# Reordering the launch and the stretch between attention and MLP, and loading wq and wk in joined rows

## The chip, the cores and the metric

The kernel runs on one core of a Trainium2 chip. The core has a matrix engine, TensorE (PE, with its weight loads shown apart as PEld), three engines for elementwise work, VectorE (DVE), ScalarE (ACT) and GpSimd (POOL), and SyncE (SP), which here only issues transfers between the device memory and the core's memory. The metric is the device time of one execution in microseconds (us), the median over several runs.

## The reference

Two equal layers, each a linear attention block and a GELU MLP, both on a layer-normalized input and with a residual. S = 2048 tokens, D = 448, 16 heads of 28, F = 1792.

```python
_layernorm = (x - mean) / sqrt(var + 1e-5)
phi = lambda t: where(t > 0, t + 1, exp(t)) + 1e-6

def A(x, wqkv, wo):                       # q, k, v = heads of x @ wqkv
    pq, pk = phi(q), phi(k)
    kv  = einsum("bhsd,bhse->bhde", pk, v)
    z   = einsum("bhsd->bhd", pk)
    num = einsum("bhqd,bhde->bhqe", pq, kv)
    den = einsum("bhqd,bhd->bhq", pq, z)[..., None] + 1e-6
    return (num / den) @ wo               # heads joined again

def B(x, w1, b1, w2, b2):
    return gelu(x @ w1 + b1) @ w2 + b2    # tanh form

for layer in range(2):                    # the same weights in both
    x = x + A(layernorm(x), wqkv, wo)
    x = x + B(layernorm(x), w1, b1, w2, b2)
```

## The kernel before

**Tiles.** The 2048 tokens are 16 tiles of 128 rows (index t), in 4 blocks of 4 tiles. The 448 columns are taken in 4 chunks of 128, the last of which covers the remaining 64 rows of a weight. To keep precision, every operand of a large product is split into a "hi" part, rounded to the matmul type fp32r by a copy on ACT, and a "lo" part, the rest, by a subtraction on DVE or POOL; a product is hi·hi, hi·lo and lo·hi. In chunk 3 the 64 rows are stored twice, so that one piece holds hi in the upper half and lo in the lower. Products with wq or wk take 11 matmuls per tile: three for each of chunks 0 to 2 and two for chunk 3 (`proj`, L280).

**Order.** The schedule is written out by hand: each engine takes its instructions in the order in which the program issues them, and waits where an operand or a buffer is not ready. So the order of calls in the program is, engine by engine, the order of the work. All loads and stores are issued on SP's queue, in program order too.

**PSUM.** Of its eight banks, tag "m" has two (products with wk, `psk`; later transposes), tag "h" two (the transposes `tp` of normalized tiles in phase 1, the products with wq, `psq`; later the MLP's first product), and tag "acc" four.

**Launch (L84 to L143, L846 to L866).** SP loads x0, then the four chunks of wk, x1, the four chunks of wq and x2; x3 and x4 follow at the start of phase 1. A chunk is one transfer of 128 rows of 448 words (`load_kq`), the last chunk two of 64 rows. x0 is normalized (`stage_a`: statistics on DVE and the power on POOL; `stage_n`: the norm on DVE and on ACT a copy of the last 64 columns, `tail`), transposed on PE (`stage_b`, L236) and split (`stage_x`: XH on ACT L241, XL on DVE L242). Among this the list at L846 puts the splits of wk (`split_hi` L122, `split_lo` L129 and L132) and of wq. PE runs a few products of ones ahead of it all (`warm_up`).

**Phase 1.** A loop over the 16 tiles issues for each the tokens of `STEP` (`STEP_0` for the first tile of a layer):

| token | work |
|---|---|
| K | product with wk of tile t |
| T, X | transpose and split of tile t+1 |
| a, n | statistics and norm of later tiles |
| kp, kh, kl | phi of k, and its hi and lo part |
| s | hi and lo part of the normalized tile, `xnh` and `xnl` |
| G | 11 matmuls that add x^T·phi(k) of tile t-1 to the four "acc" banks |
| Q | product with wq of tile t |
| qp | phi of q (`eq`, L293 to L299) and its store |
| w | the last chunk of wq's split |
| bg | loads and splits of the MLP's weights |
| tu, tv, sp, ld | turning, spreading and loading of later tiles |

Six of the 16 products with wq are left over for the stretch after phase 1.

**Between attention and MLP.** The string `ORDER` (L467) lists that work, with the same few letters for each layer: m and ms make the matrix from x^T·phi(k) and the weights, qz, qs, tq and qq scale, transpose and split the phi(q) of block 0 (tiles j = 0 to 3), `o` multiplies them (L671 to L673), `la` adds the residual and takes statistics (L691), `lb` normalizes (L199, `xm`) and copies the last columns on ACT (L698), T transposes (L236) and x splits. Between these stand the left-over products Q and their phi Qp (`fill_qphi`: three activations on ACT, among them `ep` at L445, an addition on POOL at L447, and a store), with which PE is kept at work. `pre` issues the loads of phi(q) of block 1 and, in layer 0, of two pieces of the MLP's weights.

**MLP.** For each block, 14 slices of F: `mlp1` (L736 to L740), GELU, split, `mlp2` (L754 to L756), and beside it, on the other engines, the attention output of the next block. In the last block of layer 0 the weights wk and wq are loaded again, in two halves each (`stage_square`), and split whole (`split_kq`, L134) for layer 1.

Of the kernel before, what the change touches and what calls it, by code (L numbers as in the profile page):

```python
# [9 lines left out]
F32 = mybir.dt.float32  # L10
# [12 lines left out]
def linear_attn_mlp_kernel(  # L23
# [12 lines left out]
    pe, act, dve, pool, sp = nc.tensor, nc.scalar, nc.vector, nc.gpsimd, nc.sync  # L36
    x0 = x_in[0]
# [24 lines left out]
    def bank(tag, bufs, name):  # L62
        return psum.tile([128, 512], F32, name=name, tag=tag, bufs=bufs)
# [24 lines left out]
    def stage_piece(src, c, eng, s):  # L88

        if c < 3:  # L90
            eng.dma_start(s, src[c * 128:(c + 1) * 128, :])
        else:
            eng.dma_start(s[0:64], src[TL:D, :])
            eng.dma_start(s[64:128], src[TL:D, :])
        return s

    def load_kq(name, col):
        src = wqkv[:, col:col + D]
        st = [work.tile([128, 1024], F32, name="stg", tag="S", bufs=5) for h in range(2)]
        return [stage_piece(src, c, sp, st[c // 2][:, c % 2 * 512:c % 2 * 512 + D]) for c in range(4)]  # L100

    def stage_square(src):

# [16 lines left out]
    def split_hi(name, c, st):  # L120
        hi = piece(name, c if c < 3 else 6)
        act.copy(hi, st[c])  # L122
        wkq[name, c] = (hi, piece(name, 3 + c)) if c < 3 else hi

    def split_lo(name, c, st, eng):

        if c < 3:
            hi, lo = wkq[name, c]
            eng.tensor_tensor(lo, st[c], f(hi), op=OP.subtract)  # L129
        else:  # L130
            lo = wkq[name, 3][64:128]
            eng.tensor_tensor(lo, st[c][64:128], f(lo), op=OP.subtract)  # L132
# [3 lines left out]
            split_hi(name, c, st)  # L136
            split_lo(name, c, st, pool if c in ((1, 2) if name == "k" else (0, 2)) else dve)

    st_k = load_kq("k", D)
    load_x(0, 1)  # L140
    st_q = load_kq("q", 0)
    load_x(0, 2)


# [4 lines left out]
    def warm_up(n):  # L149
        for i in range(n):  # L150
            pe.matmul(warm[:, :128], ones, ones, start=True, stop=True)
# [125 lines left out]
        dve.tensor_sub(lo.rearrange("p (c i n) -> p c i n", c=4, n=32), x, f(h))  # L277


    def proj(name, key, j):  # L280
        ps = bank("m" if name == "k" else "h", 2, "ps" + name)
        o = ps[:, :D]
        b = blocks[key]
        for c in range(3):
            hi, lo = wkq[name, c]
            pe.matmul(o, b.still(b.hi, j, c), hi, start=(c == 0), stop=False)  # L286
            pe.matmul(o, b.still(b.hi, j, c), lo, start=False, stop=False)  # L287
            pe.matmul(o, b.still(b.lo, j, c), hi, start=False, stop=False)  # L288
        pe.matmul(o, b.still(b.hi, j, 3), wkq[name, 3], start=False, stop=False)
        pe.matmul(o, b.still(b.lo, j, 3), wkq[name, 3], start=False, stop=True)  # L290
        return o

    def phi(o, name, into=None):  # L293
# [62 lines left out]
    def stage_a(l, t):  # L356
        sts[l, t] = ln_stats(xt.pop((l, t)))
# [25 lines left out]
    def stage_x(l, t):  # L383
        key = ("a", l, t // 4)
        if t < TURNED[l]:
            split_x(key, t % 4)
        else:
            split_t(key, t % 4, *block(key).pieces(t % 4))
# [9 lines left out]

    ko = {}

    def stage_k(l, t):
        ko[l, t] = proj("k", ("a", l, t // 4), t % 4)

    def stage_kphi(l, t):
        o = ko.pop((l, t))
# [44 lines left out]
    def stage_g(l, t, acc):  # L450
# [16 lines left out]

    ORDER = (
# [4 lines left out]
    )  # L473
    DEFER = NT - ORDER.split().count("Q")

    STEP = "qp K T X s a kp n kh tu kl tv G bg Q ld sp"
    STEP_0 = "K T X w a kp kh n kl s Q bg ld sp", "K T X s kp kh kl a n tu Q ld sp"
    NORM = (
        ((2,), (3, 4), (5, 6), (7,), (8,), (9,), (10,), (11,), (12, 13), (14,), (15,)),
        ((5,), (6,), (7,), (8,), (9,), (10,), (11,), (12, 13), (14,), (15,)),  # L480
# [11 lines left out]
    def phase1(l, tr):  # L492
        za = consts.tile([128, D], F32, name="za", tag="za")
        acc = [bank("acc", 4, f"G{c}")[:, :D] for c in range(4)]
        for t in range(NT):
            norm = NORM[l][t] if t < len(NORM[l]) else ()
            if t == 0:
                load_to(l, NORM[l][1][-1])
            for tok in (STEP if t else STEP_0[l]).split():
                if tok == "sp":  # L500
                    for u in norm:
                        if u % 2:
                            stage_sp(l, u)
                elif tok == "ld" and t + 2 < len(NORM[l]):
                    load_to(l, NORM[l][t + 2][-1])
                elif tok == "a":
                    for u in norm:
                        stage_a(l, u)
                elif tok == "n":
                    for u in norm:  # L510
                        stage_n(l, u)
                elif tok == "tu":
                    for u in norm[:1]:
                        stage_t(l, u)
                elif tok == "tv":
                    for u in norm[1:]:
                        stage_t(l, u)
                elif tok == "w":
                    split_hi("q", 3, st_q)
                    split_lo("q", 3, st_q, dve)  # L520
                elif tok == "T" and t + 1 < NT:
                    stage_b(l, t + 1)
                elif tok == "X" and t + 1 < NT and (l == 0 or t + 1 >= 4):
                    stage_x(l, t + 1)
                elif tok == "K":
                    stage_k(l, t)
                elif tok == "qp":
                    stage_qphi()
                elif tok == "kp":
                    stage_kphi(l, t)  # L530
                elif tok == "kh":
                    stage_kh(l, t)
                elif tok == "kl":
                    stage_kl(l, t, za)
                elif tok == "s":
                    stage_s(l, t)
                elif tok == "G" and t >= 1:
                    stage_g(l, t - 1, acc)
                elif tok == "bg" and l == 0:
                    background(BG[t])  # L540
                elif tok == "Q" and t < DEFER:
                    stage_q(l, t)
            if l == 0 and t == 4:
                sp.dma_start(b1s, b1.rearrange("(c p) -> p c", p=128))
                sp.dma_start(b2b, b2[None, :].to_broadcast([128, D]))
            if t == 11:
                tr.wv = stage_square(wqkv[:, 2 * D:])
            if t == 13:
                trans_load(l, tr)
        return za, acc  # L550
# [300 lines left out]
    split_lo("k", 1, st_k, pool)  # L851
    stage_b(0, 0)
    warm_up(2)
    stage_x(0, 0)
    split_hi("k", 2, st_k)
    split_lo("k", 2, st_k, dve)
    split_hi("k", 3, st_k)
    split_lo("k", 3, st_k, pool)
    stage_a(0, 1)
    split_hi("q", 0, st_q)  # L860
    split_hi("q", 1, st_q)
    stage_n(0, 1)
    split_lo("q", 0, st_q, dve)
    split_lo("q", 1, st_q, dve)
    split_hi("q", 2, st_q)
    split_lo("q", 2, st_q, pool)  # L866

    for l in range(LAYERS):
        tr = SimpleNamespace(mp={})
# [90 lines left out]
```

## Time and profile before

| | |
|---|---|
| median of 3 runs | 883.67 us (883.59 to 883.87) |
| the profiled execution's own time | 883.35 us |
| its span in the profile | 881.6 us |
| granted TensorE clock, mean | 0.999 |
| PE, PEld | 873.2 us (99%), 773.7 us (88%) |
| DVE, ACT, POOL | 483.8 us (55%), 345.3 us (39%), 219.0 us (25%) |
| moved by DMA | 93.71 MB, 106 GB/s in the mean |

The span runs from the first to the last recorded instruction; the execution's time has a little around it. A share is busy time over the span, as a mean over all stages. In the quoted rows of the timeline stand the start in us, the mean duration of one, the engine, the line of the kernel, the operation, out<-in by the program's names, the shapes and a count; in brackets how long the engine stood idle before it and what it had waited for. In rows of the windows stand the window, its length, and for PE, PEld, DVE, ACT and POOL the busy us with the number of instructions, then the granted clock, the busy share of the DMA engines, which counts transfers in flight on each, and GB/s. Rows that begin with a transfer's direction come from the list of DMA issues: count, size of each, and the median us from issue to landing.

### The profile page before, as it was taken

The page shows a single profiled execution, that of the slowest core. Times are in us where ns is not written, and L with a number is a line of the kernel's source. Part 1 is how long each engine was busy: PE and PEld are TensorE (multiplying, and loading weights), DVE is VectorE, ACT ScalarE, POOL GpSimd, SP SyncE. Part 2 cuts the span into 40 slices and gives each one's busy share as a digit, 9 for nine tenths or more (in the row PEclk, how much of TensorE's full clock was granted, in tenths as well). Part 3 has the DMA queues.
Part 4 walks back from the last instruction along what each step waited for, and adds up shares of the span by engine and source line. Part 5 has one row for each costly group of instructions (what it writes and reads, how often), then busy time and mean ns, then how long its engine had stood idle before and what let it go on. Part 6 is the DMA issues. An engine that isn't in the chain of part 4 may idle for free.

```text
span 881.6 us, 11685 instructions
## 1 busy us (share of the span) xinstructions
PE 873.2 (99%) x4190; PEld 773.7 (88%) x4190; DVE 483.8 (55%) x946; ACT 345.3 (39%) x607; POOL 219.0 (25%) x251
## 2 busy tenths in 40 slices
PE   8999999999999999999999999999999999999998
PEld 7999988888888888888899999788888888888887
DVE  6778585658455543226477866755574473432112
ACT  5677645323223322333355664442232233223221
POOL 4366632335012102011222333220220140140000
PEclk9999999999999999999999999999999999999999
DMA  5477733624313402051145543143332323111001
GB/s 177 131 214 233 201 94 119 194 80 140 132 59 104 155 0 96 1 178 48 48 144 188 158 138 95 63 150 102 100 117 90 110 76 132 48 49 42 1 1 42
DMA packets 62762, 93.71 MB, mean 106 GB/s; under 512 B 8816, under 2 KB 57968, under 8 KB 62704
## 3 DMA queue, kind: packets, MB, share of 16 engines
q1 hardware_dynamic: 62704, 92.97, 33.4%
q8 instruction: 33, 0.54, 0.3%
q14 instruction: 25, 0.20, 0.1%
HBM read 55.65 MB, written 34.08 MB: 102 GB/s over the span
## 4 chain that ended last, share of the span: by engine, by line
PE 89%; issue 3%; DVE 3%; POOL 2%; ACT 1%; DMA 1%; SPq 0%; POOLq 0%; DVEq 0%; ACTq 0%
PE y L756 10%; PE y L755 10%; PE y L754 10%; PE hp L737 9%; PE hp L736 9%; PE hp L738 9%; PE hp L740 3%; PE hp L739 3%; PE G L458 2%; PE G L457 2%; PE psq L286 2%; PE G L456 2%; PE op L683 2%; PE psq L287 2%; PE psk L288 2%
## 5 line engine op out<-in xcount | busy, mean ns | idle before, releaser
L746 DVE TENSOR_TENSOR gl<-g,gh 128x512 fp32r<-128x512 f32 x112 | 82.7, 738 | 300.3 <-ACT gh L745 300.3
L742 ACT ACTIVATE g<-hp,b1s 128x512 f32<-128x512 f32 x112 | 77.0, 688 | 406.5 <-PE hp L740 406.5
L756 PE MATMUL y<-w2h,gl 128*128 128x448 f32 x448 | 163.8, 366 | 0.0
L755 PE MATMUL y<-w2l,gh 128*128 128x448 f32 x448 | 163.8, 366 | 0.0
L754 PE MATMUL y<-w2h,gh 128*128 128x448 f32 x448 | 163.7, 365 | 0.0
L737 PE MATMUL hp<-XH,w1l 128*128 128x512 f32 x336 | 131.7, 392 | 0.0
L736 PE MATMUL hp<-XH,w1h 128*128 128x512 f32 x336 | 131.3, 391 | 0.0
L738 PE MATMUL hp<-XL,w1h 128*128 128x512 f32 x336 | 131.2, 390 | 0.0
L193 POOL TENSOR_TENSOR brs<-bve,mhalf 128x1 f32<-128x1 f32 x64 | 39.1, 612 | 272.3 <-DVE bve L191 269.6
L754 PEld LDWEIGHTS y<-w2h,gh 128*128 128x128 f32 x448 | 84.2, 188 | 8.9
L755 PEld LDWEIGHTS y<-w2l,gh 128*128 128x128 f32 x448 | 84.2, 188 | 8.3
L756 PEld LDWEIGHTS y<-w2h,gl 128*128 128x128 f32 x448 | 84.2, 188 | 6.5
L738 PEld LDWEIGHTS hp<-XL,w1h 128*128 128x128 f32 x336 | 63.1, 188 | 13.6
L737 PEld LDWEIGHTS hp<-XH,w1l 128*128 128x128 f32 x336 | 63.1, 188 | 11.1
L736 PEld LDWEIGHTS hp<-XH,w1h 128*128 128x128 f32 x336 | 63.2, 188 | 11.0
L745 ACT CAST gh<-g 128x512 fp32r<-128x512 f32 x112 | 69.7, 622 | 3.6
L395 POOL TENSOR_TENSOR xnl<-x,xnh 128x384 fp32r<-128x384 f32 x32 | 35.0, 1094 | 87.4 <-ACT xnh L394 57.2
L633 POOL TENSOR_TENSOR pz<-pq,zb 128x448 f32<-128x448 f32 x32 | 36.6, 1147 | 79.7 <-DVE dn L639 70.6
L740 PE MATMUL hp<-XL,w1x 128*128 128x512 f32 x112 | 43.6, 389 | 0.0
L739 PE MATMUL hp<-XH,w1x 128*128 128x512 f32 x112 | 43.6, 389 | 0.0
L277 DVE TENSOR_TENSOR XL<-sp,XH 128x512 fp32r<-128x512 f32 x50 | 41.8, 842 | 3.3 <-ACT XH L276 3.2
L702 POOL TENSOR_TENSOR x<-x,b2b 128x448 f32<-128x448 f32 x32 | 41.9, 1334 | 0.0
(144 smaller groups left out, 1564.6 us busy)
## 6 DMA issues: line engine op xcount, KB each, us to landing
x<-in_A_x_dram SPq DMA_DIRECT2D x32, 224.0 KB, 3.7
pq_d<-eq SPq DMA_DIRECT2D x32, 224.0 KB, 2.5
pq<-pq_d SPq DMA_DIRECT2D x32, 224.0 KB, 3.2
x<-x_d SPq DMA_DIRECT2D x32, 224.0 KB, 3.3
sq_a<-sq SPq DMA_DIRECT2D x13, 512.0 KB, 2.9
sp<-sq_a SPq DMA_DIRECT2D x52, 128.0 KB, 3.0
sq_q<-sq SPq DMA_DIRECT2D x12, 512.0 KB, 2.6
sp<-sq_q SPq DMA_DIRECT2D x48, 128.0 KB, 2.9
```

The lines of the kernel that those rows point to most:

```text
L702: pool.tensor_tensor(xt[l, t], xt[l, t], b2b, op=OP.add)
L736: pe.matmul(o, w1h[:, c, s], x.moving(x.hi, c), start=(c == 0), stop=False)
L737: pe.matmul(o, w1l[:, c, s], x.moving(x.hi, c), start=False, stop=False)
L738: pe.matmul(o, w1h[:, c, s], x.moving(x.lo, c), start=False, stop=False)
L739: pe.matmul(o, w1x[:, s], x.moving(x.hi, 3), start=False, stop=False)
L740: pe.matmul(o, w1x[:, s], x.moving(x.lo, 3), start=False, stop=True)
L742: act.activation(g, hp, AF.Gelu_apprx_tanh, bias=b1s[:, i:i + 1])
L745: act.copy(gh, g)
L746: dve.tensor_sub(gl, g, f(gh))
L754: pe.matmul(acc[j], gh[:, s], w2h[:, i], start=first, stop=False)
L755: pe.matmul(acc[j], gh[:, s], w2l[:, i], start=False, stop=False)
L756: pe.matmul(acc[j], gl[:, s], w2h[:, i], start=False, stop=last)
```

## The change

Three things are done together. Line numbers in the changed file are 3 to 12 higher.

1. *Loads.* `load_qk` loads each chunk of wq and wk in one transfer, with rows of 896 words that hold the q and the k columns (they lie side by side in wqkv), where there were two transfers of rows of 448 words. The order on SP's queue is now x0, chunks 0 and 1, x1, chunks 2 and 3, x2.
2. *Launch and first steps.* The split of wq leaves the list of the launch and stands whole in step 0, as token w, behind the split X of tile 1. The statistics of x1 go ahead of the split of x0, its norm behind the hi part of wk's chunk 2; the low part of wk's chunk 3 goes from POOL to DVE. The product K of tile 0 is cut into Ka (chunks 0 and 1) and Kb (chunks 2 and 3) with the transposes of tile 1 between them; K of tile 1 moves into step 0, ahead of Q; in step 1 of layer 0, Q stands at its head, ahead of T of tile 2.
3. *`ORDER`.* Behind o1, the third Qp and pre move back behind lb0, la1 and qq3; lb0 and lb1 come earlier against la1 and la2; x2 stands ahead of lb3.

```diff
@@ -94,10 +94,13 @@
             eng.dma_start(s[64:128], src[TL:D, :])
         return s
 
-    def load_kq(name, col):
-        src = wqkv[:, col:col + D]
-        st = [work.tile([128, 1024], F32, name="stg", tag="S", bufs=5) for h in range(2)]
-        return [stage_piece(src, c, sp, st[c // 2][:, c % 2 * 512:c % 2 * 512 + D]) for c in range(4)]
+    def load_qk(cs):
+
+        for c in cs:
+            st = work.tile([128, 1024], F32, name="stg", tag="S", bufs=5)
+            stage_piece(wqkv[:, :2 * D], c, sp, st[:, :2 * D])
+            st_q.append(st[:, :D])
+            st_k.append(st[:, D:2 * D])
 
     def stage_square(src):
 
@@ -136,9 +139,10 @@
             split_hi(name, c, st)
             split_lo(name, c, st, pool if c in ((1, 2) if name == "k" else (0, 2)) else dve)
 
-    st_k = load_kq("k", D)
+    st_q, st_k = [], []
+    load_qk((0, 1))
     load_x(0, 1)
-    st_q = load_kq("q", 0)
+    load_qk((2, 3))
     load_x(0, 2)
 
 
@@ -277,17 +281,19 @@
         dve.tensor_sub(lo.rearrange("p (c i n) -> p c i n", c=4, n=32), x, f(h))
 
 
-    def proj(name, key, j):
-        ps = bank("m" if name == "k" else "h", 2, "ps" + name)
-        o = ps[:, :D]
+    def proj(name, key, j, o=None, cs=range(4)):
+        if o is None:
+            o = bank("m" if name == "k" else "h", 2, "ps" + name)[:, :D]
         b = blocks[key]
-        for c in range(3):
-            hi, lo = wkq[name, c]
-            pe.matmul(o, b.still(b.hi, j, c), hi, start=(c == 0), stop=False)
-            pe.matmul(o, b.still(b.hi, j, c), lo, start=False, stop=False)
-            pe.matmul(o, b.still(b.lo, j, c), hi, start=False, stop=False)
-        pe.matmul(o, b.still(b.hi, j, 3), wkq[name, 3], start=False, stop=False)
-        pe.matmul(o, b.still(b.lo, j, 3), wkq[name, 3], start=False, stop=True)
+        for c in cs:
+            if c < 3:
+                hi, lo = wkq[name, c]
+                pe.matmul(o, b.still(b.hi, j, c), hi, start=(c == 0), stop=False)
+                pe.matmul(o, b.still(b.hi, j, c), lo, start=False, stop=False)
+                pe.matmul(o, b.still(b.lo, j, c), hi, start=False, stop=False)
+            else:
+                pe.matmul(o, b.still(b.hi, j, 3), wkq[name, 3], start=False, stop=False)
+                pe.matmul(o, b.still(b.lo, j, 3), wkq[name, 3], start=False, stop=True)
         return o
 
     def phi(o, name, into=None):
@@ -398,8 +404,8 @@
 
     ko = {}
 
-    def stage_k(l, t):
-        ko[l, t] = proj("k", ("a", l, t // 4), t % 4)
+    def stage_k(l, t, cs=range(4)):
+        ko[l, t] = proj("k", ("a", l, t // 4), t % 4, ko.get((l, t)), cs)
 
     def stage_kphi(l, t):
         o = ko.pop((l, t))
@@ -467,14 +473,15 @@
 
     ORDER = (
         "Q ld1 z ld0 ld2 qz0 qz1 G gt qs1 Q Qp kv qs0 tq1 Q mask qz2 tq0 qs2 ld3 "
-        "m0 qq1 Qp m1 qz3 ms0 qq0 m2 ms1 m3 ms2 tq2 ms3 qs3 o0 la0 qq2 o1 Qp tq3 pre "
-        "lb0 qq3 o2 la1 T0 la2 o3 lb1 x0 T1 Q lb2 la3 x1 T2 Q lb3 x2 Qp "
+        "m0 qq1 Qp m1 qz3 ms0 qq0 m2 ms1 m3 ms2 tq2 ms3 qs3 o0 la0 qq2 o1 tq3 lb0 la1 qq3 Qp pre "
+        "o2 T0 lb1 la2 o3 x0 T1 Q lb2 la3 x1 T2 Q x2 lb3 Qp "
         "T3 x3 Qp Q Qv "
     )
     DEFER = NT - ORDER.split().count("Q")
 
     STEP = "qp K T X s a kp n kh tu kl tv G bg Q ld sp"
-    STEP_0 = "K T X w a kp kh n kl s Q bg ld sp", "K T X s kp kh kl a n tu Q ld sp"
+    STEP_0 = "Ka T Kb X w K1 a kp kh n kl s Q bg ld sp", "K T X s kp kh kl a n tu Q ld sp"
+    STEP_1 = "qp Q T X s a kp n kh tu kl tv G bg ld sp", STEP
     NORM = (
         ((2,), (3, 4), (5, 6), (7,), (8,), (9,), (10,), (11,), (12, 13), (14,), (15,)),
         ((5,), (6,), (7,), (8,), (9,), (10,), (11,), (12, 13), (14,), (15,)),
@@ -496,7 +503,7 @@
             norm = NORM[l][t] if t < len(NORM[l]) else ()
             if t == 0:
                 load_to(l, NORM[l][1][-1])
-            for tok in (STEP if t else STEP_0[l]).split():
+            for tok in (STEP_0[l] if t == 0 else STEP_1[l] if t == 1 else STEP).split():
                 if tok == "sp":
                     for u in norm:
                         if u % 2:
@@ -516,14 +523,19 @@
                     for u in norm[1:]:
                         stage_t(l, u)
                 elif tok == "w":
-                    split_hi("q", 3, st_q)
-                    split_lo("q", 3, st_q, dve)
+                    split_kq("q", st_q)
                 elif tok == "T" and t + 1 < NT:
                     stage_b(l, t + 1)
                 elif tok == "X" and t + 1 < NT and (l == 0 or t + 1 >= 4):
                     stage_x(l, t + 1)
                 elif tok == "K":
                     stage_k(l, t)
+                elif tok == "Ka":
+                    stage_k(l, t, (0, 1))
+                elif tok == "Kb":
+                    stage_k(l, t, (2, 3))
+                elif tok == "K1":
+                    stage_k(l, 1)
                 elif tok == "qp":
                     stage_qphi()
                 elif tok == "kp":
@@ -851,19 +863,13 @@
     split_lo("k", 1, st_k, pool)
     stage_b(0, 0)
     warm_up(2)
+    stage_a(0, 1)
     stage_x(0, 0)
     split_hi("k", 2, st_k)
+    stage_n(0, 1)
     split_lo("k", 2, st_k, dve)
     split_hi("k", 3, st_k)
-    split_lo("k", 3, st_k, pool)
-    stage_a(0, 1)
-    split_hi("q", 0, st_q)
-    split_hi("q", 1, st_q)
-    stage_n(0, 1)
-    split_lo("q", 0, st_q, dve)
-    split_lo("q", 1, st_q, dve)
-    split_hi("q", 2, st_q)
-    split_lo("q", 2, st_q, pool)
+    split_lo("k", 3, st_k, dve)
 
     for l in range(LAYERS):
         tr = SimpleNamespace(mp={})
```

## The prediction

> **What bounds the kernel now.** I read the shares of the engines first, then who TensorE (PE) waited for, then the stages, and then the launch and the stretch between the halves row by row. The page's engine shares:
>
> ```profile
> PE 873.2 (99%) x4190; PEld 773.7 (88%) x4190; DVE 483.8 (55%) x946; ACT 345.3 (39%) x607; POOL 219.0 (25%) x251
> ```
>
> PE is busy for 99% of the span. Nothing is gained off it, and the only time an order can win or lose is where PE stands still. The view of PE's waits names those places; its columns are the total, the times and the longest, in us:
>
> ```profile
> PE tp L236 <- DVE xm L199: 1.5, 2, 0.7
> ...
> PE psq L286 <- ACT ep L445: 0.8, 2, 0.4
> ...
> PE G L458 <- POOL xnl L395: 0.3, 1, 0.3
> ```
>
> The first two happen twice, once in each layer, between attention and MLP; the others belong to the launch. The launch by windows, two stretches of it and the whole (the last column is what the DMAs moved, in GB/s):
>
> ```profile
> 2.00:10.00 8.00, 7.62 (x37) 6.61 (x36) 4.11 (x10) 3.64 (x8) 3.00 (x4) 1.00 0.96 278
> 12.00:13.00 1.00, 1.00 (x7) 0.94 (x6) 0.70 (x2) 1.00 (x3) 0.81 (x1) 1.00 1.07 389
> 0.00:18.00 18.00, 15.69 (x73) 12.85 (x73) 10.34 (x23) 10.45 (x20) 7.54 (x19) 1.00 0.65 191
> ```
>
> PE idles 2.3 us in the launch (18.00 less 15.69) and waits 2.3 us between the halves in both layers together (1.5 and 0.8); the granted clock is 1.00. So the change works on two small accounts, and I price each.
>
> **Between the halves.** PE's own list is the same before and after; only the lists of ACT, DVE, POOL and SP move. The rows there:
>
> ```profile
> 126.16 1.14 POOL L447 TENSOR_TENSOR eq<-ep,eq 128x448 f32<-128x448 f32 x1
> ```
> ```profile
> 126.22 1.32 DVE L199 TENSOR_SCALAR xm<-x,bmv,brs 128x448 f32<-128x448 f32 x1
> 128.35 0.69 DVE L661 TENSOR_TENSOR ql<-tq,qh 112x512 fp32r<-112x512 f32 x1 [0.80 <-ACT qh L660]
> 128.95 0.61 DVE L691 TENSOR_TENSOR x<-op,x 128x448 f32<-128x448 f32 x1
> ...
> 130.56 0.62 DVE L691 TENSOR_TENSOR x<-op,x 128x448 f32<-128x448 f32 x1
> ...
> 132.17 0.51 DVE L199 TENSOR_SCALAR xm<-x,bmv,brs 128x448 f32<-128x448 f32 x1
> ```
> ```profile
> 131.71 0.37 PE L673 MATMUL op<-Mh,ql 112*128 112x448 f32 x1
> 132.82 0.63 PE L236 MATMUL tp<-ident,xm 128*128 128x128 f32 x4 [0.74 <-DVE xm L199]
> ...
> 135.52 0.60 PE L236 MATMUL tp<-ident,xm 128*128 128x128 f32 x4
> ...
> 139.18 0.47 PE L286 MATMUL psq<-wq,XH 128*128 128x448 f32 x1 [0.39 <-ACT ep L445]
> ```
> ```profile
> 137.51 0.25 ACT L698 COPY xm<-xm 128x64 f32<-128x64 f32 x1 [2.11 <-DVE xm L199]
> ...
> 138.58 0.55 ACT L445 ACTIVATE ep<-psq 128x448 f32<-128x448 f32 x1
> ```
>
> T1 (132.82) stood 0.9 us behind o3 (131.71 plus a step of 0.20) because its norm, lb1, came at 132.17. lb1 was late for two reasons. The norm before it (lb0, 126.22) took 1.32 us beside the POOL addition of Qp, against 0.51 for the next one; and the sum of tile 2 (130.56) stood ahead of it. The change puts lb0 and la1 ahead of that Qp and lb1 ahead of la2. Worked out: lb0 126.22 to 126.73; la1's sum and statistics take 1.61 (128.95 to 130.56), to 128.34; ql of qq3 (0.60 from 128.35 to the next row), with POOL's power beside it; lb1 at 129.0. The addition of Qp now falls beside lb1, so I give it the 1.32 again: 130.3, and 0.3 for ACT's copy (as at 137.51). PE wants T1 at 131.91: 1.3 us of slack. T1's whole 0.91 goes. Next late is the last Q, which at 139.18 began 0.60 after ACT's ep (138.58) had begun. In the new order that chain starts at T2, 0.91 earlier at 134.6: 0.64 to XH and 0.67 to XL (rows of the launch, below), 0.6 for XL and 0.5 for lb3 on DVE, now in that order, to 137.0; from the copy at 137.51 to ep at 138.58 are 1.07, with a cast of half a microsecond between, which now comes earlier: ep at 137.7, the last Q at 138.3. Gain 0.9 per layer, about **1.85 us for two**. Ends: 0 (the new stall takes all) and 2.3 (all waits go). SP's loads in pre now issue behind Qp's store; the data is first read behind the last Q, so that stretch of PE work covers them; without it POOL's first pz, beside the MLP, would be late.
>
> **The launch.** Here PE's list changes. Before: K0, T1, Q0, K1, T2, G0, Q1, K2, T3, G1. After: half K0, T1, half K0, K1, Q0, Q1, T2, G0, K2, T3, G1, with wq split only after K0. Matmuls are neither added nor removed. Two new waits decide. First, K1, Q0 and what follows need the last chunk of wk, which now rides with wq: ten tiles of 224 KB (x0, x1 and eight of weights) must be in, where five did before.
>
> ```profile
> x<-in_A_x_dram SPq DMA_DIRECT2D x32, 224.0 KB, 3.7
> ```
> ```profile
> 8.29 0.57 ACT L122 CAST wk<-stg 128x448 fp32r<-128x448 f32 x1 [0.38 <-DMA stg<-in_A_wqkv_dram]
> ...
> 12.06 0.59 ACT L241 CAST XH<-tp 128x512 fp32r<-128x512 f32 x1
> 12.55 0.57 ACT L122 CAST wq<-stg 128x448 fp32r<-128x448 f32 x1
> ```
> ```profile
> 10.18 0.48 PE L289 MATMUL psk<-wk,XH 128*128 128x448 f32 x1 [0.28 <-POOL wk L132]
> ...
> 10.50 0.36 PE L290 MATMUL psk<-wk,XL 128*128 128x448 f32 x1
> ```
>
> Call the landing L. Ten tiles are 2.29 MB; at the 278 GB/s of the window from 2 to 10 us they are in at 10.2. The old cast of the same last bytes at 12.55 shows no wait on a DMA, so 12.55 is the late end for the same bytes. At the 389 GB/s of the window from 12 to 13 it would be 7.9. I take **L = 11.3**, between the first two, nearest to rows of these very loads. [...]
>
> From L: the cast of wk chunk 3 (0.57) ends at 11.9, DVE's low part of it (0.62, as at 13.40 below; it was POOL's, and PE's 10.18 followed that) at 12.6. PE takes chunk 3 in 0.52 (10.18, 10.50, plus a step), so K1 starts at 13.1. K1, Q0, Q1 are 33 matmuls at 0.203 (21 of them fill 25.36 to 29.62, below): T2 could start at 19.8.
>
> Second: T2 writes a bank of tag h. With Q1 moved ahead of it, the two banks hold Q0 and Q1, so T2 waits until DVE has read Q0 (eq0). That chain starts with the q split, which the second layer does in just this order already:
>
> ```profile
> 407.09 1.97 ACT L122 CAST wq<-stg 128x448 fp32r<-128x448 f32 x4
> ```
> ```profile
> 408.15 1.26 DVE L129 TENSOR_TENSOR wq<-stg,wq 128x448 fp32r<-128x448 f32 x1 [0.24 <-ACT wq L122]
> 409.44 1.46 DVE L132 TENSOR_TENSOR wq<-stg,wq 64x448 fp32r<-64x448 f32 x1
> ```
>
> DVE's two low parts take 1.26 and 1.46 beside POOL's, not 0.62, and end 3.81 after ACT's first cast. The first q cast comes two steps of 0.49 (12.06, 12.55) behind that of wk chunk 3: 12.3; so DVE ends the split at 16.1. From there on by the old rows:
>
> ```profile
> 13.40 0.62 DVE L132 TENSOR_TENSOR wq<-stg,wq 64x448 fp32r<-64x448 f32 x1
> ...
> 18.15 0.62 DVE L299 SCALAR_TENSOR_TENSOR eq<-psq,eq 128x448 f32<-128x448 f32 x1 [0.60 <-ACT eq L297]
> 18.69 0.68 DVE L242 TENSOR_TENSOR XL<-tp,XH 128x512 fp32r<-128x512 f32 x1
> ...
> 23.53 0.62 DVE L419 SCALAR_TENSOR_TENSOR kl<-psk,kh 128x448 fp32r<-128x448 f32 x1 [0.90 <-ACT kh L412]
> ```
> ```profile
> 18.02 0.57 ACT L241 CAST XH<-tp 128x512 fp32r<-128x512 f32 x1
> ...
> 25.36 0.58 ACT L241 CAST XH<-tp 128x512 fp32r<-128x512 f32 x1 [0.82 <-PE tp L236]
> ```
> ```profile
> 24.72 0.49 PE L236 MATMUL tp<-ident,x 128*128 128x128 f32 x3
> ...
> 25.36 0.36 PE L457 MATMUL G<-kl,xnh 128*128 128x448 f32 x1
> ...
> 29.62 0.37 PE L286 MATMUL psk<-wk,XH 128*128 128x448 f32 x1
> ```
>
> Split end 14.02 to eq0 18.15 is 4.13: eq0 runs 20.26 to 20.88, T2 starts at 20.9 (a stall of 1.1). T to XH 0.64 (24.72, 25.36), XH to XL 0.67 (18.02, 18.69): XL at 22.2. From XL to the end of kl of tile 1 are 5.46 (18.69 to 23.53, and 0.62): 27.7. PE would reach G1's second matmul, which reads kl, at 26.6 (22 matmuls, and 0.6 for each of T2 and T3, behind 20.9), so another 1.1 is lost. Before, kl ended at 24.15 and the matmul ran at 25.36, with 1.2 to spare. From there to K3 is 4.26 (25.36 to 29.62) and 0.1 to restart: K3 at 32.1 against 29.62. **The launch loses 2.5 us**, or L less 8.8. From K3 on both orders are the same and PE had no wait. The old launch stall at xnl (0.3) does go, but these come in its place.
>
> **The sum.** 2.5 less 1.85 is +0.65 us. The profiled execution took 883.35 (span 881.6 and 1.7 around it), which makes 884.0. The median of the runs is 883.67, 0.32 above it, so **884.3**. L from 10.2 to 12.55 gives 883.2 to 885.6.
>
> **The rivals.** *Long rows stream.* At 389 GB/s wk chunk 1 (five tiles) is in by 4.9 and the last chunk by 7.9. Then the chain of x1 binds, for POOL's low part of wk chunk 1 now stands ahead of x1's power:
>
> ```profile
> 5.57 0.30 ACT L366 COPY tail<-x 128x128 f32<-128x128 f32 x1 [1.14 <-DVE x L362]
> ```
> ```profile
> 6.98 1.14 POOL L129 TENSOR_TENSOR wk<-stg,wk 128x448 fp32r<-128x448 f32 x1 [1.99 <-ACT wk L122]
> ...
> 10.21 0.56 POOL L193 TENSOR_TENSOR brs<-bve,mhalf 128x1 f32<-128x1 f32 x1
> ```
>
> Tail 0 ends at 5.9 as before, the cast of chunk 1 (0.57) at 6.4, POOL's 1.14 and 0.56 at 8.2, the norm (0.51) at 8.7, and 0.64 later XH of T1 at 9.4, which in the sum is L and 0.53: as L = 8.9. The launch breaks even, and the whole gives 883.67 + 0.1 - 1.85 = 881.9. For it: half as many packets; against it: the row from 2 to 10 us has x0 and x1, which lie in one piece, in its 278 GB/s too. Chance 0.12. *The gain between the halves is given back*: ends on the slow side. Qp's addition now falls beside lb1; if lb1 and its copy end after 131.9 T1 stalls as before, and with all the gain lost the result is 883.67 + 2.5 = 886.2. For it, 1.32 against 0.51 in the rows; against it, 1.3 us of slack. Chance 0.09. *Slow landing*: if long rows keep one DMA engine behind and L reaches 13.2, the launch loses 4.4: 886.2. Chance 0.07. *The clock falls*: PE, which has nothing from its last warm-up product until XH0, and little until 12.6, could be granted a lower clock. If K1 and half of Q0 (17 matmuls) took twice the step of 0.203, that is 3.4 more, less the 1.1 that T2 waits anyway: 886.6. The row of 0 to 18 us shows 1.00 through the old gaps. Chance 0.04. [...] That the loads don't become long rows is small: it is the late end of L.
>
> **How the numbers follow.** My forecast has 0.68, nearly all of it within 0.2% (1.77 us, about what a measurement of this kernel can tell from no change). The streaming case lies at the edge of that, half of its spread counted faster; the other three lie outside on the slow side, less their near halves. Faster 0.07, same 0.75, slower 0.18. The range, 882.4 to 886.0, holds the forecast, the near part of the streaming case and the near part of the two at 886.2.
>
> **What would show it.** Right: no wait of T1 for xm in either layer, the wait for ep near 0.6; T2 of tile 2 waiting about 1 us for eq, G of tile 1 about 1 us for kl; wk chunk 3 cast near 11.3; K3 near 32. Wrong: T2 or G1 without a wait, the cast before 10 or after 12.6, T1 still waiting, or a granted clock under 1.00 in the launch.

## The result, and the profile after

The changed kernel takes 885.73 us in the median of 16 runs (883.68 to 888.94), the kernel before beside it 883.77 (16 runs, 883.14 to 885.08). The ratio is 1.0022, with a 95% interval of 1.0014 to 1.0031: slower by 0.14 to 0.31%, which lies across the 0.2% that I had called the bound of what can be told. Foreseen was a change of +0.63 us from the 883.67 us known then; measured are +1.96. The profiled execution took 884.98 us, with a span of 883.3; before it was 883.35 and 881.6, so these two profiles show 1.63 us of the 1.96 between the medians.

The page's engine shares:

```profile
PE 872.6 (99%) x4190; PEld 773.7 (88%) x4190; DVE 485.6 (55%) x946; ACT 345.1 (39%) x607; POOL 219.0 (25%) x251
```

PE does the same work (4190 rows); what was added is standing still. Who PE waited for (total, times, longest):

```profile
PE psk L291 <- ACT XH L245: 1.7, 1, 1.7
...
PE psk L295 <- DVE wk L135: 0.9, 1, 0.9
PE tp L240 <- DVE eq L305: 0.8, 1, 0.8
PE psq L291 <- ACT ep L451: 0.7, 2, 0.4
...
PE G L462 <- ACT kh L418: 0.6, 1, 0.6
...
PE G L463 <- DVE kl L425: 0.2, 1, 0.2
```

The row of tp waiting for xm is gone; the wait for ep is left; tp now waits for eq, and G for kh and kl. The launch by windows, as before:

```profile
0.00:18.00 18.00, 13.37 (x65) 11.46 (x66) 9.77 (x20) 7.90 (x15) 6.44 (x17) 1.00 0.66 191
```

PE is busy for 13.37 us of the first 18 where it was 15.69. The view of the chain that ended last has the last chunk of the weights at the head of it, from its issue at 3.73:

```profile
3.73 8.46 DMA stg<-in_A_wqkv_dram
12.27 0.56 ACT wk L125
```

The chain of the launch in the timeline, in the order of the prediction's steps:

```profile
12.27 0.56 ACT L125 CAST wk<-stg 128x448 fp32r<-128x448 f32 x1 [0.85 <-DMA stg<-in_A_wqkv_dram]
...
14.06 0.37 PE L291 MATMUL psk<-wk,XH 128*128 128x448 f32 x1
...
15.53 1.47 DVE L135 TENSOR_TENSOR wq<-stg,wq 64x448 fp32r<-64x448 f32 x1
...
21.18 0.62 DVE L305 SCALAR_TENSOR_TENSOR eq<-psq,eq 128x448 f32<-128x448 f32 x1 [0.67 <-ACT eq L303]
...
21.86 0.55 PE L240 MATMUL tp<-ident,x 128*128 128x128 f32 x3 [0.82 <-DVE eq L305]
...
28.02 0.62 DVE L425 SCALAR_TENSOR_TENSOR kl<-psk,kh 128x448 fp32r<-128x448 f32 x1 [0.90 <-ACT kh L418]
...
33.05 0.37 PE L291 MATMUL psk<-wk,XH 128*128 128x448 f32 x1
```

The cast of wk chunk 3 begins at 12.27, K of tile 1 at 14.06, DVE ends the q split at 17.0, eq of tile 0 begins at 21.18, T of tile 2 at 21.86, kl of tile 1 ends at 28.64, K of tile 3 begins at 33.05, 3.43 us later than before.

Between the halves of layer 0:

```profile
132.56 1.33 DVE L203 TENSOR_SCALAR xm<-x,bmv,brs 128x448 f32<-128x448 f32 x1
```
```profile
135.27 0.37 PE L685 MATMUL op<-Mh,ql 112*128 112x448 f32 x1
135.48 0.60 PE L240 MATMUL tp<-ident,xm 128*128 128x128 f32 x4
...
141.81 0.47 PE L291 MATMUL psq<-wq,XH 128*128 128x448 f32 x1 [0.36 <-ACT ep L451]
```

T1 (135.48) stands one step behind the last product of o3 (135.27). From the last G of phase 1 (106.70 before, 110.26 after) to the last Q (139.18, 141.81) are now 31.55 us instead of 32.48; layer 1 gives the same two numbers. So the ledger of the two profiles is: launch and phase 1 +3.56, of which 3.43 by K of tile 3; the two stretches between the halves -1.86; rest -0.07.

### The profile page after: what moved, and what is told of

Read it like the earlier page. It is cut to its first block, busy times and chain, and to the rows that moved or that the text cites. A ratio compares the mean times of both kernels' runs of the same rounds, so it can differ in the third digit from the quotient of the medians.

```text
span 883.3 us, 11679 instructions
## 1 busy us (share of the span) xinstructions
PE 872.6 (99%) x4190; PEld 773.7 (88%) x4190; DVE 485.6 (55%) x946; ACT 345.1 (39%) x607; POOL 219.0 (25%) x251
## 4 chain that ended last, share of the span: by engine, by line
PE 95%; DVE 2%; ACT 1%; DMA 1%; SPq 0%; issue 0%; POOL 0%; ACTq 0%; DVEq 0%; POOLq 0%
PE y L768 10%; PE y L767 10%; PE y L766 10%; PE hp L749 9%; PE hp L748 9%; PE hp L750 9%; PE hp L751 3%; PE hp L752 3%; PE G L463 2%; PE G L464 2%; PE G L462 2%; PE psq L291 2%; PE psq L293 2%; PE psq L292 2%; PE psk L293 2%; PE psk L291 2%
## 5 line engine op out<-in xcount | busy, mean ns | idle before, releaser
L191 DVE BATCH_NORM_STATS2 bst<-x 128x6 f32<-128x448 f32 x64 | 39.9, 623 | 5.5 <-DMA x<-in_A_x_dram 4.4
```

## The experiments

My theory was that the launch is one chain that begins when the last chunk of wk is in, so that K of tile 3 comes a fixed time after that, and that ORDER's gain is independent of it. The kernels ran in several groups, not all on one chip, so each is compared with the kernel before as it ran in its own group.

**The two halves of the change apart.** First ORDER alone (the part of the string that differs):

```diff
 # kernel before
-o1 Qp tq3 pre lb0 qq3 o2 la1 T0 la2 o3 lb1 x0 T1 Q lb2 la3 x1 T2 Q lb3 x2 Qp
+o1 tq3 lb0 la1 qq3 Qp pre o2 T0 lb1 la2 o3 x0 T1 Q lb2 la3 x1 T2 Q x2 lb3 Qp
```

> The kernel before with the new ORDER string and nothing else. My theory: the two stretches between the halves gain 0.92 us each and the launch is untouched, so 883.77 - 1.9 = 881.9 us (ratio 0.998), no wait of PE for xm, K of tile 3 still near 29.6 us, and a spread of single runs as narrow as that of before. Rival: the gain exists only because the changed launch shifts the other engines' work against PE; then T1 waits for xm as before and the time stays at 883.8.

Measured: 881.02 us against 883.08, ratio 0.9982 (0.9973 to 0.9990). K of tile 3 at 29.22. In the timeline of PE:

```profile
131.52 0.60 PE L236 MATMUL tp<-ident,xm 128*128 128x128 f32 x4
...
137.85 0.47 PE L286 MATMUL psq<-wq,XH 128*128 128x448 f32 x1 [0.36 <-ACT ep L445]
```

From the last G (106.30) to the last Q are 31.55 us here too, T1 without a wait. The gain is real, is ORDER's own, and the launch has no part in it. Single runs spread over 2.4 us (880.57 to 882.94), as those of the kernel before beside it did (882.35 to 884.67), so a spread of that size needs no new launch. Then the rest alone, with the old ORDER:

> The changed kernel with the old ORDER string: loads, launch and first steps are changed, the stretch between the halves is not. Theory: K of tile 3 near 33.05 us, both waits for xm back at 0.9 us, so 883.77 + 3.6 = 887.4 us (ratio 1.004), with single runs that scatter as widely as those of the changed kernel, because the landing of the last weight chunk is on the path. Rival (the launch's loss is partly hidden later): under 886.5.

Measured: 887.78 against 883.08, ratio 1.0051 (1.0039 to 1.0064), single runs 885.79 to 889.57. Both waits for xm are back. That is 4.7 us and not 3.6. The profiled execution is the slowest of the six (889.57): in it the cast began at 12.59 and K of tile 3 came at 34.11, 21.5 us later and not 20.8, and phase 1 of layer 1 was 1.6 us longer (both below). The two ratios fit with two parts that add up: 1.0022 for both over 0.9982 for ORDER is 1.0040, at the low end of the interval measured here.

**Does the launch hang on the landing?** The load of x2 moved ahead of the last two chunks:

```diff
-    load_qk((2, 3))
     load_x(0, 2)
+    load_qk((2, 3))
```

> The changed kernel with the load of x2 moved ahead of chunks 2 and 3 of the weights: same work, the last chunk of wk lands one tile of 224 KB later. Theory (the launch is a chain that begins at that landing): the cast of wk chunk 3 moves from 12.27 us to about 13.0 (224 KB at the 304 GB/s of the window from 6 to 9 us of the kernel before are 0.75 us), and every later step by the same: end of the q split 17.75, K of tile 3 33.8; 0.75 us over the changed kernel at a full clock. Rival (the q split's price or the T wait alone sets the end): K of tile 3 stays at 33.0 to 33.2.

Measured: 886.39 against 883.51, ratio 1.0030 (1.0017 to 1.0042). In the timeline of ACT and PE:

```profile
13.64 0.56 ACT L125 CAST wk<-stg 128x448 fp32r<-128x448 f32 x1 [1.60 <-DMA stg<-in_A_wqkv_dram]
...
34.60 0.36 PE L291 MATMUL psk<-wk,XH 128*128 128x448 f32 x1
```

The landing moved by 1.37 us instead of 0.75, and K of tile 3 by 1.55: later by what the load was later, and 0.18 more (this profile has a stretch at half the clock, below). The next kernels give more points of the same line.

**The length of the rows.** Each chunk in two transfers of 448-word rows, q ahead of k, so that wk's last bytes stay last:

```diff
-            stage_piece(wqkv[:, :2 * D], c, sp, st[:, :2 * D])
-            st_q.append(st[:, :D])
-            st_k.append(st[:, D:2 * D])
+            st_q.append(stage_piece(wqkv[:, :D], c, sp, st[:, :D]))
+            st_k.append(stage_piece(wqkv[:, D:2 * D], c, sp, st[:, D:2 * D]))
```

> The changed kernel with every chunk loaded in two transfers with rows of 448 words, q ahead of k, in the same order of chunks: only the length of the rows is undone, and the last bytes of wk are still the last of the weights. Theory: the row length does nothing, the cast of wk chunk 3 begins near 12.2 us, K of tile 3 near 33.0, 885.7 us, within 0.3 us of the changed kernel. Rival A, long rows hold the last landing back: the cast near 11.4, 884.9 us. Rival B, long rows help: the cast after 12.8, 886.4 us or more.

Measured: 884.70 against 883.08, ratio 1.0016 (1.0007 to 1.0025), an interval that overlaps that of the changed kernel.

```profile
11.62 0.56 ACT L124 CAST wk<-stg 128x448 fp32r<-128x448 f32 x1 [1.54 <-DMA stg<-in_A_wqkv_dram]
...
32.42 0.36 PE L290 MATMUL psk<-wk,XH 128*128 128x448 f32 x1
```

The cast came 0.65 us earlier and K of tile 3 with it (0.63), as rival A had it and not as I had. One profile does not tell a rule from a scatter, so I did it again with the clock held (below).

**The clock.** The changed kernel's runs had mean granted clocks from 0.994 to 1.000, ten of the 16 at 0.998 or less, and most of the slow ones were among them (median of the ten 886.40, of the other six 884.59). I put ten products of ones into PE's gaps, five of them where two stood already; this kernel is called the filled one below. The edit in short, without the conditions that keep it to the launch:

```diff
-    warm_up(2)
+    warm_up(7)      # behind the transposes of tile 0
...
+    warm_up(2)      # K of tile 0: ahead of the first product with XL
+    warm_up(3)      # K of tile 0: ahead of chunk 3
```

> The changed kernel with ten more products of ones that go nowhere, put into PE's gaps of the launch: five more behind the transposes of tile 0, two ahead of the first product with XL, three ahead of chunk 3 of K of tile 0. Each takes 0.3 us and lies in a wait. Theory (the wide scatter and the lower mean clock of half the runs of the changed kernel come from these gaps): all runs have a mean clock of 0.999 or 1.000, none is above 886.5, the median falls from 885.7 to 884.7, and the profiled times of the steps stay within 0.3 us. Rival (the scatter is that of the landings): clocks of 0.994 to 0.998 and times to 888 stay.

Measured: 11 of 12 clocks 0.999 or more and one 0.998, and no run above 886.39; but the median is 885.48 (against 883.51; ratio 1.0018, 1.0009 to 1.0028), not 884.7. The clock was held and the highest runs went, but the median hardly moved: there my theory fell. Five of the profiles have the clock at 0.50 in the launch: for 3.41 us in three of them (x2 first, and old loads and new loads under the old launch, both below), for 6.83 in one (launch alone) and for 10.24 in one (Q of tile 1 behind G, below). The windows view of four kernels, cut into windows of 3.41 us from the first moment at which the clock is recorded, shows how busy PE was before it fell (length, PE's busy time, clock, DMA share, GB/s). The changed kernel:

```profile
5.44:8.85 3.41, 1.71 (x14) 1.00 1.02 320
```

Launch alone:

```profile
7.80:11.21 3.41, 1.61 (x7) 1.00 1.05 231
11.21:14.62 3.41, 2.90 (x10) 0.50 0.74 227
14.62:18.04 3.42, 3.42 (x10) 0.50 0.01 2
18.04:21.45 3.41, 3.41 (x18) 1.00 0.00 0
```

With x2 first:

```profile
11.07:14.48 3.41, 1.22 (x5) 1.00 0.86 228
14.48:17.89 3.41, 2.98 (x8) 0.50 0.02 8
```

With Q of tile 1 behind G (below):

```profile
5.42:8.84 3.42, 1.35 (x13) 1.00 1.02 298
8.84:12.25 3.41, 2.71 (x6) 0.50 1.05 190
```

In the changed kernel PE was busy for 1.71 of the 3.41 us, and the clock of the next window (8.85 to 12.27) was 1.00. Behind the windows with 1.61 (launch alone), 1.22 (x2 first) and 1.35 (Q of tile 1 behind G) it was 0.50. With the launch alone it was 0.50 once more behind a window with 2.90 and 1.00 behind one with 3.42; with x2 first it was back behind 2.98, for the mean clock of that execution, 0.998, leaves room for one such window only. These are readings of one profile each, and what sets the clock they do not show. Yet the price of the lower clock can be small, because PE had been waiting in that stretch anyway: the next pair shows it.

**What the new steps cost.** Q of tile 1 behind G of tile 0 again:

```diff
-    STEP_1 = "qp Q T X s a kp n kh tu kl tv G bg ld sp", STEP
+    STEP_1 = "qp T X s a kp n kh tu kl tv G bg Q ld sp", STEP
```

> The changed kernel with Q of tile 1 behind G of tile 0 again, as in the kernel before, so that T of tile 2 writes a bank that is free. Theory: the wait of T for eq (0.99 us) goes, but G of tile 0 comes too early for the low part of the normalized tile on POOL (xnl, till 21.2) and waits for it 1.5 to 2 us instead; the two waits of G of tile 1 (1.1 together) go. K of tile 3 near 32.5 instead of 33.05: 0.5 us less than the changed kernel. Rival (Q of tile 1 ahead of T is the cause of the loss): 2 us less, K of tile 3 near 31.

Measured: 884.72 against 883.51, ratio 1.0009 (0.9998 to 1.0020). The profile fell into an execution with a late landing (cast at 14.03) and half the clock from 8.84 to 19.08; K of tile 3 came at 34.27, 20.24 us behind the cast. The same with the ten products of ones:

> The changed kernel with the ten products of ones in its gaps and with Q of tile 1 behind G of tile 0, so that the look at this order is not clouded by a lower clock. In the other profiles of the new launch K of tile 3 came 20.8 us behind the cast of wk chunk 3. Theory: that distance shrinks by 0.5 us, to 20.3, because G of tile 0 then waits for xnl where T of tile 2 had waited for eq; 885.0 us where the filled kernel with the new order takes 885.5. Rival (Q of tile 1 ahead of T of tile 2 is the larger part of what the new steps cost): the distance falls to 19.3 or less, and the time by 1.5 us or more.

Measured: 885.11 against 883.16, ratio 1.0020 (1.0011 to 1.0029).

```profile
11.01 0.56 ACT L125 CAST wk<-stg 128x448 fp32r<-128x448 f32 x1 [0.95 <-DMA stg<-in_A_wqkv_dram]
...
19.99 0.47 PE L468 MATMUL G<-kh,xnl 128*128 128x448 f32 x1 [0.41 <-POOL xnl L405]
...
31.28 0.36 PE L291 MATMUL psk<-wk,XH 128*128 128x448 f32 x1
```

20.27 us behind the cast, at the full clock, where the other order has 20.8: the order of Q and T is worth 0.5 us, as the theory said, and G of tile 0 waits for xnl in exchange. And 20.24 with three windows at half the clock against 20.27 with none: there the clock cost nothing. In the kernel with the launch alone two windows cost 0.7 (21.5 against 20.8); I take it that PE's extra Q ahead of T used up the slack, which no run shows by itself. So in these profiles a falling clock is more a sign that PE stood waiting than what the waiting cost. How much of the 1.8 us between the two groups of the changed kernel's runs is the clock and how much late landings isn't shown, since the landing is on record for one run of each kernel alone.

**Rows once more, on one chip and with the clock held.** The filled kernel with short and with long rows:

> The changed kernel with the ten products of ones in its gaps, and each chunk loaded in two transfers with rows of 448 words, q ahead of k. With the clock held, only the length of the rows differs from the kernel with the products of ones alone. In the profiles so far the last weight chunk was in at 12.19, 12.50 and 12.50 us (13.95 in one) with long rows and at 11.34 to 12.20 with short ones. Theory (long rows land later at the last engine): the last chunk in by 11.7, K of tile 3 near 32.5 instead of 33.3, the median 0.8 us under that of the kernel with long rows. Rival (the landings differ only from run to run): medians within 0.3 us of each other.

> The changed kernel with the ten products of ones in its gaps, as before, beside the same with short rows on one chip. Both theories: 885.2 to 885.7 us, all clocks 0.998 or more, the last weight chunk in near 12.5 and K of tile 3 near 33.3.

Measured: 885.20 (ratio 1.0021, 1.0012 to 1.0030) and 886.50 (1.0029, 1.0017 to 1.0041) against 882.97. The medians are 1.3 us apart, long rows slower, and the second lies above what I had expected. But the profiles had their casts at 11.72 and 11.99 and K of tile 3 only 0.20 apart; of the 1.8 us between the two profiled executions (884.41 and 886.2) 1.6 are a longer phase 1 of layer 1, for which the loads of the launch are no known reason. Over all profiles in which ten tiles were ahead, the last weight chunk was in at 11.34 to 12.20 us with short rows (six profiles, median 11.7) and at 10.93 to 13.95 with long ones (seven, median 12.5). Long rows scatter more and come rather later, but the intervals of the two times overlap, and the earliest landing of all was one of long rows: a loss by the length itself is possible and not shown, and a gain is not seen. Long rows that stream, with the last chunk in by 7.9, were not seen: the earliest of the seven was in at 10.93.

The line on which all this lies, for the seven profiles of the new launch and Q ahead of T:

| kernel | cast of wk chunk 3 | K of tile 3 | distance |
|---|---|---|---|
| short rows | 11.62 | 32.42 | 20.80 |
| filled, short rows | 11.72 | 32.60 | 20.88 |
| filled, again | 11.99 | 32.80 | 20.81 |
| the changed kernel | 12.27 | 33.05 | 20.78 |
| filled | 12.58 | 33.40 | 20.82 |
| launch alone (clock at half for two windows) | 12.59 | 34.11 | 21.52 |
| x2 first (clock at half for one) | 13.64 | 34.60 | 20.96 |

And what comes behind K of tile 3 is the same for all: from there to the end of the span are 850.0 to 850.4 us in each of the twelve profiles with the new ORDER but one (filled, again: 851.7, with the longer phase 1). So a later K of tile 3 goes whole into the time.

**Loads and launch crossed.** The old loads under the new launch:

> The changed kernel with the old loads: wk, then x1, then wq, each chunk by itself; launch list, steps and ORDER stay changed. Theory 1, the landing of the last wk chunk sets K of tile 1, and once it lands near 8.3 us the norm of x1 and its tail (ACT near 10.8, ahead of the cast of wk chunk 3 on the same engine) set it, about 1.0 us ahead of the changed kernel: K of tile 1 near 13.1, end of the q split near 16.0, K of tile 3 near 32.0, 884.7 us. So most of the launch's loss stays, because the order of the steps (q split whole, Q of tile 1 ahead of T of tile 2) costs it too. Theory 2, the order of landing makes the whole loss: K of tile 3 near 29.6 and 882.0 us.

Measured: 884.63 against 883.08, ratio 1.0019 (1.0010 to 1.0027); K of tile 1 at 13.32, the q split's end at 15.96, K of tile 3 at 32.04. DVE, then ACT and PE in that profile:

```profile
8.15 0.63 DVE L187 BATCH_NORM_STATS2 bst<-x 128x6 f32<-128x448 f32 x1 [2.00 <-DMA x<-in_A_x_dram]
...
9.10 0.68 DVE L242 TENSOR_TENSOR XL<-tp,XH 128x512 fp32r<-128x512 f32 x1
```
```profile
10.41 0.30 ACT L368 COPY tail<-x 128x128 f32<-128x128 f32 x1 [2.91 <-DVE x L364]
10.61 0.57 ACT L122 CAST wk<-stg 128x448 fp32r<-128x448 f32 x1
...
32.04 0.36 PE L287 MATMUL psk<-wk,XH 128*128 128x448 f32 x1
```

The statistics of x1, now ahead of XL of tile 0 in DVE's order, wait for the landing of x1 (8.15), and XL behind them comes at 9.10 instead of 7.47. The last chunk of wk is in at 7.55, but its cast stands behind the copy of x1's last columns and begins at 10.61. Theory 1 holds: with wk in early, the chain begins at x1. And the new loads under the old launch, with the new ORDER:

> The kernel before with the new ORDER and with the new loads (chunks with rows of 896 words, x1 behind two of them), but with the old launch and steps. Theory: the cast of wk chunk 3 begins near 12.5 us; its low part on POOL (1.14) stands ahead of the power of x1, so the norm of x1 comes near 15, T of tile 1 near 15.7 instead of 11.1 and K of tile 3 near 33.8 instead of 29.2: 4.5 us over the kernel with the new ORDER alone, near 885.5 (more where the clock falls). Then the loads are what costs, and the new launch takes 0.5 to 1 us of that back. Rival (the old launch is simply the better order, whatever the loads): under 884.5.

Measured: 886.85 against 882.97, ratio 1.0036 (1.0024 to 1.0049).

```profile
13.31 1.13 POOL L135 TENSOR_TENSOR wk<-stg,wk 64x448 fp32r<-64x448 f32 x1 [4.46 <-ACT wk L125]
...
15.12 0.51 DVE L366 TENSOR_SCALAR x<-x,bmv,brs 128x448 f32<-128x448 f32 x1 [3.06 <-POOL brs L197]
...
15.68 0.80 PE L240 MATMUL tp<-ident,x 128*128 128x128 f32 x3 [0.52 <-DVE x L366]
...
34.29 0.36 PE L290 MATMUL psk<-wk,XH 128*128 128x448 f32 x1
```

POOL's low part of wk chunk 3, then the norm of x1, then T of tile 1 at 15.68, as written; K of tile 3 at 34.29. So K of tile 3 stands at 29.2 with old loads and old launch, 32.0 with the new launch, 34.3 with the new loads, 33.05 with both. The new launch takes back 1.2 us of what the new loads cost, and costs 2.8 by itself. These differences are rough: the profiles at 32.0 and at 34.3 have one window at half the clock each (from 10.91 and from 15.83), the other two none, and at 32.0 the distance from the cast is 21.4 us and not 20.8.

**A version faster than before and after.** ORDER, and two small edits of the old launch that go at its waits for x1 and for xnl:

```diff
     split_hi("k", 3, st_k)
-    split_lo("k", 3, st_k, pool)
     stage_a(0, 1)
+    split_lo("k", 3, st_k, dve)
...
-    STEP_0 = "K T X w a kp kh n kl s Q bg ld sp", ...
+    STEP_0 = "K T X w s a kp kh n kl Q bg ld sp", ...
```

> The kernel before with the new ORDER, and two edits of the old launch: the statistics of x1 ahead of the low part of wk chunk 3, which goes from POOL to DVE; and s (hi and lo of the normalized tile 0) right behind w in step 0. Theory: ORDER is worth 1.9 us, the first edit lets T of tile 1 start 0.3 to 0.5 us earlier, the second takes away the wait of G of tile 0 for xnl (0.55 us in the profile of the kernel with the new ORDER alone): 880.1 to 880.4 us on a chip where the kernel before takes 883.1, ratio 0.9967. Rival (the waits only move on): no better than ORDER alone, ratio 0.998.

Measured: 880.44 us against 883.51, ratio 0.9961 (0.9945 to 0.9976); single runs 880.17 to 880.88.

```profile
16.77 0.45 PE L456 MATMUL G<-kh,xnh 128*128 128x448 f32 x1
...
17.26 0.36 PE L458 MATMUL G<-kh,xnl 128*128 128x448 f32 x1
...
28.44 0.37 PE L286 MATMUL psk<-wk,XH 128*128 128x448 f32 x1
```

G's first product with xnl (17.26) follows without a wait, where ORDER alone had waited 0.39, and PE's wait for the norm of x1 went from 0.51 to 0.29. K of tile 3 stands at 28.44, 0.8 ahead of ORDER alone (29.22). The interval overlaps that of ORDER alone, so that the time is better than with ORDER alone is shown by one profile and not by the medians.

## Why the prediction was right, and where not

The forecast of 884.3 us is 1.4 below the median, which lies inside the range (882.4 to 886.0), near its slow end. The direction was right; the size of the change was three times the foreseen. The range held with 0.3 us to spare, because its slow end allowed for the old row of 12.55 us (885.6) and for a part of the rivals at 886.2.

*Between the halves.* Foreseen 1.85 us for two layers, measured 1.86. T1 lost its wait, lb1 was foreseen with 1.32 us beside Qp's addition, took 1.33 and ended with slack, and the last Q kept its wait for ep, beginning 0.59 after it. This step held in every part.

*The launch.* The structure held: the chain from the cast of wk chunk 3 through K1, the q split on DVE, eq, T2, kl and G1 to K of tile 3 was put at 20.8 us, and measured between 20.8 and 20.9 wherever the clock was full. T2's stall was 1.0 (foreseen 1.1), those of G1 together 1.1 (1.1), though the first half of them was for kh, which I had not named. I had also not seen that the cast of wk chunk 1, which waits for its long transfer until 7.4, stands on ACT ahead of XH of tile 0, and I had not priced the statistics of x1, which now stand on DVE ahead of XL. PE waited 1.7 and 0.7 us for these, but both lie ahead of the wait for the last chunk, which began the chain in any case.

*What failed is one term: L.* I took 11.3 for the landing, between a rate and an old row, and the cast began at 12.27. Every step behind it came late by 0.9 to 1.0 us. The nearest row was the one that I had put at the late end: the same bytes in the kernel before, whose cast at 12.55 showed no wait; the trace has these bytes in at 12.20 before and at 12.19 after. What the rate missed shows in the same trace: it has 16 signals for the landing of a transfer, as many as the DMA engines that the profile's page counts. For the last chunk the ninth came at 10.6 us, near the 10.2 of the rate, but the sixteenth at 12.19, and the cast began 0.08 behind that one. With L at 12.27 my own sum gives 884.3 + 0.97 = 885.3, 0.4 from the median. The other profiles point the same way: the median landing of the seven with long rows is 12.5, and long rows brought no gain over rows of 1,792 B.

*The rivals.* Streaming rows did not come. The gain between the halves was not given back. Slow landing is half right: the last chunk came in as late as 13.95 in one profile. That this scatter is why single runs spread from 883.7 to 888.9 is likely in part and not shown: with the clock held the two series of the filled kernel end at 886.39 and 887.02, and the kernel before, which has wk in at 8.2, spreads over 1.9 us too. The falling clock I gave a chance of 0.04 and a price of 2.3 us. A clock under 1.00 in the launch was one of my signs of being wrong; the profiled execution did not have it, but ten of the 16 runs had a mean clock of 0.994 to 0.998. Of all profiles, those with means of 0.993 to 0.998 had one to three windows at half the clock in the launch and those with 0.999 or 1.000 none, so I read the ten as runs in which it fell. In the profiles it cost nothing to 0.7 us. My price counted on a doubled step, 0.41 us; at the 0.50 from 15.83 to 19.24 of the new loads under the old launch the products followed each other by 0.37. My reason against it, the 1.00 in the row of 0 to 18 us, was a reading of the old order, in which PE idled 2.3 of the 18 us; in the new one it idled 4.6, and in other profiles of this launch the clock was 0.50 behind windows of 3.41 us with 1.22 to 1.61 busy.

*Not settled.* The two profiles differ by 1.63 us and the medians by 1.96; how much of these 0.3 us is later landings in other runs, how much the clock, and how much the longer step told of below, no run separates.

## What to carry to other kernels

Before a launch is reordered, write down for each new order which landing its chain begins at, and price that landing by the row that moved the same bytes, not by a mean rate: here the user waited for the last of 16 signals, which came at 12.19 us where the ninth came at 10.6. Joining two transfers made the first user of either wait for both: the last chunk of wk, in at 8.20 us in the kernel before, came in with the last of wq at 12.19. And when a change bundles parts, try them apart: ORDER alone was 0.18% faster, the whole 0.22% slower.

## What the runs showed of the hardware

- In five profiles PE's clock went from 1.00 to 0.50, behind windows of 3.41 us in which PE was busy for 1.61 (launch alone), 1.35 (old loads; Q of tile 1 behind G), 1.22 (x2 first) and 0.81 us (new loads under the old launch); behind one with 1.71 (the changed kernel) it was 1.00. It was back at 1.00 behind windows with 2.98 (x2 first) and with 3.41 or 3.42 busy (the other four), and still at 0.50 behind 2.90 (launch alone) and 2.71 and 2.59 (Q of tile 1 behind G). In none of the five did PE stand idle for the whole window before the fall: it was idle for 1.8 to 2.6 us of it. The ends of matmuls are modelled in the profile, and so are these busy times. What sets the clock the runs do not show. One kernel has runs with and without it: the mean clocks of the changed kernel go from 0.994 to 1.000.
- Rows of 3,584 B brought no gain over rows of 1,792 B: a packet took 140 ns in the median of the changed kernel's trace against 74 in that of the kernel before (packets begun in the first 10 us), and the landing of the last weight chunk scattered over 3.0 us instead of 0.9.
- A landing has 16 signals in the trace, and the cast that waited for the last weight chunk began 0.08 to 0.09 us behind the last of them (seven profiles with long rows). Half of the signals for that chunk were there by 10.2 to 11.0 us with long rows and by 10.3 to 11.1 with short ones, and the last came 0.4 to 3.4 us later with long rows and 0.7 to 1.3 with short ones (seven and six profiles; the eighth at 10.50 and the last at 12.19 in the changed kernel, at 11.11 and 12.20 in the kernel before).
- In two profiles (launch alone; filled, again) phase 1 of layer 1 was 1.6 us longer at a full clock and without a wait: the products of phase 1 in layer 1 followed each other by 0.207 us instead of 0.203. Why isn't known.
